# Local attention and a gated projection in one kernel: scores in four 64x64 products, transposes by 64 rows, three banks for dense work

## The chip, the cores and the metric

The kernel runs on one core of a Trainium2 chip. The metric is device time in microseconds (us) of one execution. Before the change it was 435.26 us, the median of 3 runs (435.07 to 436.68).

## The reference

Attention with batch 4, 8 heads, 768 positions and 64 features a head comes first. A query sees 31 neighbours (distance under 16) and 24 summaries, one for each 32 positions: the maximum of the keys and the mean of the values. A gated projection follows.

```python
k_sum = k.reshape(B, H, nb, block, D).max(axis=3)          # block 32
v_sum = v.reshape(B, H, nb, block, D).mean(axis=3)
scores_l = where(|i - j| < 16, q @ k.T / 8, -1e9)
scores_s = q @ k_sum.T / 8 + log(32)
a = softmax(concat([scores_l, scores_s])) ; attn = a @ concat([v, v_sum])
h = relu(x @ w_in)                                          # x: 4 x 768 x 512, w_in 512 x 1024
u, v = halves of h ; v_n = layer norm of v
v_s = w_spatial @ v_n + b_spatial[:, None]                  # w_spatial 768 x 768
out = (u * v_s) @ w_out                                     # w_out 512 x 512
```

The arithmetic is float32. Each dense product is made as three products of float32 values split into a high and a low part (hh, hl, lh), and w_in and w_out come in as 64-bit floats, which the kernel splits itself.

## The kernel before

**Attention.** The work is cut into 24 groups: 4 batches, 3 stretches of 256 queries (`c`), and 2 sets of four heads (`g`). A group has two head pairs (`pr`), and the two heads of a pair lie on partitions 0 to 63 and 64 to 127 (`a`). A stretch has four blocks of 64 queries (`BPU`), and a block is scored against 120 columns (`KW`): 64 keys, 24 summaries and 32 more keys. The steps of a group:

- `scores` (L410), once for each pair: for each block one product for each head, 64 features by 64 queries against 120 columns, so 8 products. TensorE runs each float32 product in two passes, and the profile shows 16 records for a pair and 32 for a group. The output of a pair is one PSUM bank (tile `s`; two such banks).
- softmax: per block VectorE (DVE) adds the mask and takes the extreme (L419), ScalarE (ACT) takes the exponent (L423), then come the sum's inverse (L428, L429) and the scaling (L431, on DVE or on GpSimd, called POOL).
- `trans` (L442), once for each pair: four transposes of 128 rows by 120 columns into one bank (tile `t`), copied to SBUF (tile `pt`) by ACT or DVE in one go (L229).
- `mix` (L458): 16 products with the values into tile `x`, one half of the output partitions for each head; 32 records.

**Dense work.** For each batch: `pv` (projection to v, 6 pieces), `pu` (to u, 8), `sp` (`w_spatial`, 8) and `po` (output, 6). All of their matmuls stand in one helper and have line L491. Each piece fills one bank of a pool of four (`m`), which ACT or DVE empties.

**What sets the order.** Nothing is left to a scheduler on the chip. The program lists operations with costs, and a planner (`Plan.order`) simulates the engines once, picks at each step the operation that can start first, and so writes the instruction order of every engine. The constants near the end steer it: `PACE` (time from group to group), `DENSE_0` and `STRETCH` (when dense pieces come due), `WIN_V` to `WO_AT` (weight loads), `FAVOUR` and `BUSY` (how far POOL is preferred over DVE for the operations that both can run), `RATE` and `WIRE` (speed and delay of loads). All loads go out on SyncE's queue. On the chip each engine runs its list strictly in order and waits where an input isn't there.

**The head of the program.** Keys, queries, values and the first half of w_in come in first; warming matmuls (`warm`) fill TensorE until there is work. `vsum` (L363) needs a 1.5 MB load of values (`vn`), and the first `mix` needs `vsum`.

**The end.** The last output piece is copied out of PSUM in two column halves of 256, first by DVE (L579) and then by ACT (L580), and goes out on two queues.

Of the kernel before, what the change touches and what calls it, by code (L numbers as in the profile page):

```python
# [63 lines left out]
class Plan:  # L64


    SLOTS = dict(s=2, t=1, x=1, m=4, k=4, vt=1, p=4, pt=3, x01h=2, x01l=2, x2h=2, x2l=2, g=NG, e=3, u=1, vnh=1, vnl=1,
                 gm=2, st=8, bs=4, mv=4)
# [6 lines left out]
    def add(self, engs, fn, pri, w=(), r=(), port=False, xfer=0):  # L75
# [103 lines left out]
def tile_local_summary_attention_gmlp(ctx: ExitStack, tc: tile.TileContext, qT, kext, vpad, vnat, vT, w_in, w_sp, b_rep, w_out, maskc, out):  # L179
# [220 lines left out]
    def scores(u, pri):  # L400
        b, c, pr = u
        ps = Buf(ps_s, [P, 512], F32, "s", f"s{b}_{c}_{pr}")
        kt, (qt, buf) = k_sb[b, pr], q_sb.pop(u)

        def mm(e):
            for i in range(BPU):
                g = c * BPU + i
                for a in range(2):
                    hs = slice(a * D, (a + 1) * D)
                    nc.tensor.matmul(  # L410
                        out=ps.t[hs, i * KW:(i + 1) * KW], lhsT=qt[hs, i], rhs=kt.t[hs, g * SEG:g * SEG + KW],
                        start=True, stop=True)
# [22 lines left out]
    def trans(u, pri):  # L435
        b, c, pr = u
        ps = Buf(ps_t, [P, 512], F32, "t", f"t{b}_{c}_{pr}")
        pt = p_sb.pop(u)

        def mm(e):  # L440
            for i in range(BPU):
                nc.tensor.transpose(out=ps.t[:KW, i * P:(i + 1) * P], in_=pt.t[:, i, :], identity=ident)  # L442
# [123 lines left out]
    def proj_out(b, t, pri):  # L566
# [8 lines left out]
        if (b, t) == (B - 1, NT - 1):  # L575
            hf = DM // 2

            def last(e):
                nc.vector.tensor_copy(out=ob.t[:, hf:], in_=ps.t[:, hf:])  # L579
                nc.scalar.copy(out=ob.t[:, :hf], in_=ps.t[:, :hf])  # L580
# [170 lines left out]
```

## Time and profile before

| | |
|---|---|
| median of 3 runs | 435.26 us |
| the profiled execution | 436.41 us, its span 434.6 us |
| mean granted TensorE clock | 0.995 |
| busy: TensorE matmul / weight load | 425.7 / 353.7 us |
| busy: DVE / ACT / POOL | 265.6 / 221.7 / 45.6 us |
| HBM read / written | 40.16 / 6.29 MB |

The span is the time from the first to the last instruction; 1.8 us of the profiled execution lie around it, and this execution took 1.15 us more than the median. In the profile PE is TensorE's matmul side and PEld its weight loads, which overlap it. A PE that is busy is not a PE at its peak: matmuls are pipelined, so what a block of work costs is read from the starts of the instructions around it.

### The profile page before, as it was taken

The page shows a single profiled execution, that of the slowest core. Times are in us where ns is not written, and L with a number is a line of the kernel's source. Part 1 is how long each engine was busy: PE and PEld are TensorE (multiplying, and loading weights), DVE is VectorE, ACT ScalarE, POOL GpSimd, SP SyncE. Part 2 cuts the span into 40 slices and gives each one's busy share as a digit, 9 for nine tenths or more (in the row PEclk, how much of TensorE's full clock was granted, in tenths as well). Part 3 has the DMA queues.
Part 4 walks back from the last instruction along what each step waited for, and adds up shares of the span by engine and source line. Part 5 has one row for each costly group of instructions (what it writes and reads, how often), then busy time and mean ns, then how long its engine had stood idle before and what let it go on. Part 6 is the DMA issues. An engine that isn't in the chain of part 4 may idle for free.

```text
span 434.6 us, 8979 instructions
## 1 busy us (share of the span) xinstructions
PE 425.7 (98%) x3374; PEld 353.7 (81%) x3374; DVE 265.6 (61%) x921; ACT 221.7 (51%) x668; POOL 45.6 (10%) x65
## 2 busy tenths in 40 slices
PE   8979999999999999999999999999999999999996
PEld 7637787788898888888888988789788988898885
DVE  4858999989993948455581657365482437143322
ACT  5658985874574546554273346375263254231121
POOL 1033611210001013010000002100000002010000
PEclk9989999999999999999999999999999999999999
DMA  8998967242155832320143251102103000000021
GB/s 288 362 271 289 296 205 247 76 133 60 26 165 161 250 118 60 106 67 26 38 144 118 87 186 27 38 24 62 38 26 109 26 36 15 0 2 0 2 97 48
DMA packets 25867, 47.03 MB, mean 108 GB/s; under 512 B 2528, under 2 KB 12896, under 8 KB 25696
## 3 DMA queue, kind: packets, MB, share of 16 engines
q1 hardware_dynamic: 25680, 46.33, 33.7%
q8 instruction: 26, 0.43, 0.4%
q14 instruction: 17, 0.14, 0.1%
q10 hardware_dynamic: 144, 0.13, 0.1%
HBM read 40.16 MB, written 6.29 MB: 107 GB/s over the span
## 4 chain that ended last, share of the span: by engine, by line
PE 82%; DMA 8%; DVE 8%; SPq 1%; issue 0%; ACT 0%; ACTq 0%
PE sp L491 24%; PE po L491 15%; PE pu L491 13%; PE pv L491 12%; PE s L410 8%; PE x L458 4%; PE t L442 4%; DMA vn<-in_vnat_dram 3%; DMA k<-in_kext_dram 2%; PE vsum L363 2%; DMA qd<-in_qT_dram 1%; DMA vt<-in_vT_dram 1%; DMA ws<-in_w_sp_dram 1%; DVE gm L342 1%; DVE p L419 1%; DVE p L431 1%
## 5 line engine op out<-in xcount | busy, mean ns | idle before, releaser
L423 ACT ACTIVATE p<-p,sums 128x120 f32<-128x120 f32 x192 | 73.6, 386 | 8.0 <-DVE sums L419 7.8
L491 PE MATMUL sp<-wsp_h,vnh 128*128 128x512 f32 (+1 forms) x192 | 66.7, 348 | 0.0
L491 PE MATMUL sp<-wsp_l,vnh 128*128 128x512 f32 (+1 forms) x192 | 64.7, 337 | 0.0
L491 PE MATMUL sp<-wsp_h,vnl 128*128 128x512 f32 (+1 forms) x192 | 64.6, 336 | 0.0
L419 DVE CUSTOM_DVE_ANT_0 p<-s,mask 128x120 f32<-128x120 f32 x192 | 42.8, 276 | 12.4 <-PE s L410 12.2
L491 PE MATMUL po<-wo_h,gt 128*128 128x512 f32 x128 | 47.7, 402 | 0.0
L410 PE MATMUL s<-k,qd 64*64 64x120 f32 x768 | 45.9, 267 | 0.5 <-DMA qd<-in_qT_dram 0.5
L410 PEld LDWEIGHTS s<-k,qd 64*64 64x64 f32 x768 | 39.1, 133 | 7.7 <-issue 4.4
L491 PE MATMUL pu<-xh,win_h 128*128 128x512 f32 (+1 forms) x128 | 44.7, 349 | 0.0
L491 PE MATMUL pu<-xh,win_l 128*128 128x512 f32 (+1 forms) x128 | 43.1, 337 | 0.0
L491 PE MATMUL pu<-xl,win_h 128*128 128x512 f32 (+1 forms) x128 | 43.1, 336 | 0.0
L562 ACT CAST gt<-g 128x512 fp32r<-128x512 f32 (+1 forms) x32 | 16.3, 513 | 50.2 <-DVE g L554 50.1
L491 PEld LDWEIGHTS sp<-wsp_h,vnh 128*128 128x128 f32 x192 | 36.4, 189 | 5.1 <-issue 1.3
L491 PE MATMUL pv<-win_h,xh 128*128 128x512 f32 x96 | 39.8, 414 | 0.0
L491 PEld LDWEIGHTS sp<-wsp_h,vnl 128*128 128x128 f32 x192 | 36.4, 189 | 3.9
L472 DVE TENSOR_TENSOR xl<-x,xh 128x512 fp32r<-128x512 f32 x24 | 16.4, 685 | 37.7 <-ACT xh L471 37.7
L491 PEld LDWEIGHTS sp<-wsp_l,vnh 128*128 128x128 f32 x192 | 36.4, 190 | 3.5
L491 PE MATMUL pv<-win_l,xh 128*128 128x512 f32 x96 | 37.6, 391 | 0.0
L491 PE MATMUL pv<-win_h,xl 128*128 128x512 f32 x96 | 37.5, 391 | 0.0
L491 PE MATMUL po<-wo_l,gt 128*128 128x512 f32 x96 | 37.5, 391 | 0.0
L553 DVE TENSOR_TENSOR g<-sp,brep 128x512 f32<-128x512 f32 (+1 forms) x32 | 17.7, 554 | 31.5 <-PE sp L491 22.1
L229 ACT COPY pt<-t 120x512 f32<-120x512 f32 x40 | 23.4, 584 | 26.1 <-PE t L442 25.9
(103 smaller groups left out, 784.7 us busy)
## 6 DMA issues: line engine op xcount, KB each, us to landing
k<-in_kext_dram SPq DMA_DIRECT2D x16, 544.0 KB, 5.8
qd<-in_qT_dram SPq DMA_DIRECT2D x24, 256.0 KB, 4.2
ve<-in_vpad_dram SPq DMA_DIRECT2D x24, 256.0 KB, 3.7
out_dram<-ob SPq DMA_DIRECT2D x23, 256.0 KB, 2.0
vt<-in_vT_dram SPq DMA_DIRECT2D x12, 384.0 KB, 4.0
wi<-in_w_in_dram SPq DMA_DIRECT2D x6, 512.0 KB, 5.1
ve<-in_vpad_dram SPq DMA_DIRECT2D x24, 128.0 KB, 3.4
wo<-in_w_out_dram SPq DMA_DIRECT2D x8, 256.0 KB, 5.4
```

What stands on the lines that cost most here:

```text
L229: (nc.scalar.copy if e == "ACT" else nc.vector.tensor_copy)(out=out_, in_=in_)
L342: nc.vector.tensor_reduce(out=g[:, :48].rearrange("p (s g) -> p s g", g=4), in_=kv[:, :, :QB].rearrange("p s (g e) -> p s g e", e=16), axi ...
L363: add(("PE", 860), lambda e, t=t, o=o: nc.tensor.matmul(out=ps.t[:SEG], lhsT=vs_in[:, o:o + SEG], rhs=vn.t[:, t, :], start=t == 0, stop=t ...
L410: nc.tensor.matmul(out=ps.t[hs, i * KW:(i + 1) * KW], lhsT=qt[hs, i], rhs=kt.t[hs, g * SEG:g * SEG + KW], start=True, stop=True)
L419: add(("DVE", 205), lambda e, i=i, mi=mi: nc.vector.tensor_tensor_reduce(out=pt.t[:, i, :], in0=ps.t[:, i * KW:(i + 1) * KW], in1=mask[:, ...
L423: add(("ACT", 380), lambda e, i=i: nc.scalar.activation(out=pt.t[:, i, :], in_=pt.t[:, i, :], func=AF.Exp, scale=-1.0, bias=st.t[:, 0, i:i ...
L442: nc.tensor.transpose(out=ps.t[:KW, i * P:(i + 1) * P], in_=pt.t[:, i, :], identity=ident)
L458: nc.tensor.matmul(out=ps.t[a * D:(a + 1) * D, r, n * QB:(n + 1) * QB], lhsT=ve[buf][:, n, o:o + D], rhs=tts[r].t[:, n * P + a * QB:n * P ...
L472: add(("DVE", 610), lambda e: nc.vector.tensor_sub(out=l.t[:, :, fs], in0=ps.t, in1=h.t[:, :, fs]), pri, w=[kl], r=[ps, kh, h, l])
L491: nc.tensor.matmul(out=ps.t[:, :n], lhsT=x, rhs=y, start=(j == i == 0), stop=(j == last and i == 2))
L553: add(("DVE", dve_ns(n)), lambda e: nc.vector.tensor_add(out=g.t[:, :n], in0=ps.t[:, :n], in1=brep[:, ts]), pri, w=[g], r=[ps, "brep"])
L562: add(("ACT", act_ns(n)), lambda e: nc.scalar.copy(out=gh[1](), in_=g.t[:, :n]), pri, w=[kh], r=[g, gt])
```

## The change

The four parts:

1. **Scores.** A group's two pairs are scored in one go. For each block there are four products in the order (head, pair) = (0,0), (1,1), (0,1), (1,0). The head sets the 64 rows of the array and the bank; the pair sets the 64 columns of the array and the 64 output partitions. Tile `s` is now two banks in a pool of one (it was one bank in a pool of two). The softmax takes one head of both pairs at a time.
2. **Transposes.** A softmax tile now holds pair 0 on rows 0 to 63 and pair 1 on rows 64 to 127. Each block is transposed as two products of 64 rows, which write 64 columns each to two banks, so there are 8 transposes where there were 4, per half group. The two copies to SBUF (120x512 as before) come after both halves.
3. **Banks.** Scores 2, transposes 2 (was 1), mix 1, dense pieces 3 (was 4).
4. **Plan.** New constants and costs (scores 1000 ns for a group, transposes 300 ns for a half group, mix 1050, loads at 330 GB/s), ten staging buffers for eight, some waits on staging buffers set earlier in `spatial`. The last output piece is cut by rows (64 and 64) and no longer by columns.

```diff
-    SLOTS = dict(s=2, t=1, x=1, m=4, ..., g=NG, ...)              # NG = 8
+    SLOTS = dict(s=1, t=1, x=1, m=3, ..., g=NG, ...)              # NG = 10
...
-    def scores(u, pri):
-        b, c, pr = u
-        ps = Buf(ps_s, [P, 512], F32, "s", f"s{b}_{c}_{pr}")
+    def scores(b, c, pg, buf, pri):
+        ps = Buf(ps_s, [P, 2, 512], F32, "s", f"s{b}_{c}_{pg}")
+        kts = [k_sb[b, 2 * pg + r] for r in range(2)]
+        qt = qd[buf]
...
-                for a in range(2):
+                for a, r in ((0, 0), (1, 1), (0, 1), (1, 0)):
                     hs = slice(a * D, (a + 1) * D)
                     nc.tensor.matmul(
-                        out=ps.t[hs, i * KW:(i + 1) * KW], lhsT=qt[hs, i], rhs=kt.t[hs, g * SEG:g * SEG + KW],
-                        start=True, stop=True)
-        add(("PE", 930), mm, pri, w=[ps], r=[kt, f"q{buf}"])
+                        out=ps.t[r * QB:(r + 1) * QB, a, i * KW:(i + 1) * KW], lhsT=qt[hs, r, i],
+                        rhs=kts[r].t[hs, g * SEG:g * SEG + KW], start=True, stop=True)
+        add(("PE", 1000), mm, pri, w=[ps], r=[*kts, f"q{buf}"])
+        for a in range(2):
+            softmax((b, c, pg, a), ps, pri)
...
-    def trans(u, pri):
-        ps = Buf(ps_t, [P, 512], F32, "t", f"t{b}_{c}_{pr}")
-                nc.tensor.transpose(out=ps.t[:KW, i * P:(i + 1) * P], in_=pt.t[:, i, :], identity=ident)
-        add(("PE", 450), mm, pri, w=[ps], r=[(pt, "n"), pt])
+    def trans(b, c, pg, pri):
+        ps = Buf(ps_t, [P, 2, 512], F32, "t", f"t{b}_{c}_{pg}")
+        for a in range(2):
+                    for r in range(2):
+                        hs = slice(r * QB, (r + 1) * QB)
+                        nc.tensor.transpose(out=ps.t[:KW, r, a * CH + i * QB:a * CH + (i + 1) * QB], in_=pt.t[hs, i, :], identity=ident[hs, hs])
+            add(("PE", 300), mm, pri, w=[(ps, a)], r=[(pt, "n"), pt, ps])
...
-                nc.vector.tensor_copy(out=ob.t[:, hf:], in_=ps.t[:, hf:])
-                nc.scalar.copy(out=ob.t[:, :hf], in_=ps.t[:, :hf])
+                nc.vector.tensor_copy(out=ob.t[D:], in_=ps.t[D:])
+                nc.scalar.copy(out=ob.t[:D], in_=ps.t[:D])
...
-PACE_0, PACE, DENSE_0, STRETCH = 12.13, 15.91, 66.3, 1.27
+PACE_0, PACE, DENSE_0, STRETCH = 12.13, 15.16, 59.674, 1.249
-FAVOUR, BUSY = 1380.0, 44480.0
-WIRE, RATE, RATE_64, RATE_32 = 1800, 375.0, 215.0, 195.0
+FAVOUR, BUSY = 1760.0, 55780.0
+WIRE, RATE, RATE_64, RATE_32 = 2200, 330.0, 210.0, 195.0
```

How the order moves, at three places. In the names, the batch is left out and the last number is the program's own: `s_0_0_2212` is the scores tile of stretch 0, set 0.

TensorE, the first scores of the third batch, before:

```order
L491 MATMUL pv_2_2076<-win_h,xl_01_1_1343 128x512
L410 MATMUL s_0_0_2098<-k_0_1633,qd_105 64x120 x8
L410 MATMUL s_0_1_2115<-k_1_1640,qd_105 64x120 x8
L380 MATMUL vmp_0_2125<-ident,vs_in 88x128
L380 MATMUL vmp_1_2127<-ident,vs_in 88x128
```

and after:

```order
L501 MATMUL pv_3_2189<-win_h,xl_01_1_1438 128x512
L411 MATMUL s_0_0_2212<-k_0_1866,qd_105 64x120
L411 MATMUL s_0_0_2212<-k_1_1877,qd_105 64x120 x2
L411 MATMUL s_0_0_2212<-k_0_1866,qd_105 64x120 x2
L411 MATMUL s_0_0_2212<-k_1_1877,qd_105 64x120 x2
L411 MATMUL s_0_0_2212<-k_0_1866,qd_105 64x120 x2
L411 MATMUL s_0_0_2212<-k_1_1877,qd_105 64x120 x2
L411 MATMUL s_0_0_2212<-k_0_1866,qd_105 64x120 x2
L411 MATMUL s_0_0_2212<-k_1_1877,qd_105 64x120 x2
L411 MATMUL s_0_0_2212<-k_0_1866,qd_105 64x120
L381 MATMUL vmp_0_2236<-ident,vs_in 88x128
```

Two blocks of 8 products became one of 16, in which the two pairs' keys take turns. No group's scores are parted any more, where five of the groups from the third on had other work between their two blocks.

TensorE, the transposes of the same group, before:

```order
L442 MATMUL t_0_0_2195<-ident,p_0_0_2136 120x128 x4
L491 MATMUL pu_0_1_2202<-xh_01_0_1193,win_h 128x512
L491 MATMUL pu_0_1_2202<-xl_01_0_1208,win_h 128x512
L491 MATMUL pu_0_1_2202<-xh_01_0_1193,win_l 128x512
L491 MATMUL pu_0_1_2202<-xh_01_0_1193,win_h 128x512
L491 MATMUL pu_0_1_2202<-xl_01_0_1208,win_h 128x512
L491 MATMUL pu_0_1_2202<-xh_01_0_1193,win_l 128x512
L442 MATMUL t_0_1_2213<-ident,p_0_1_2151 120x128 x4
```

and after:

```order
L450 MATMUL t_0_0_2309<-ident,p_0_0_0_2253 120x64 x8
L501 MATMUL pu_0_2_2303<-xh_01_0_1242,win_h 128x512
L501 MATMUL pu_0_2_2303<-xl_01_0_1252,win_h 128x512
L501 MATMUL pu_0_2_2303<-xh_01_0_1242,win_l 128x512
L501 MATMUL pu_0_2_2303<-xh_01_1_1422,win_h 128x512
L501 MATMUL pu_0_2_2303<-xl_01_1_1438,win_h 128x512
L501 MATMUL pu_0_2_2303<-xh_01_1_1422,win_l 128x512
L450 MATMUL t_0_0_2309<-ident,p_0_0_1_2268 120x64 x8
```

The halves of a group's transposes still stand apart with dense matmuls between them; each is 8 short ones in place of 4.

POOL, between the second group's softmax and the first layer norm, before (`wsp_l` is the low part of w_spatial, `mv` a layer norm's variance):

```order
L243 TENSOR_TENSOR wsp_l<-ws_0_311,wsp_h 128x512
L284 TENSOR_TENSOR win_l<-wf_2_0_347,wi_2_0_218 128x256
L431 TENSOR_TENSOR p_1_0_402<-p_1_0_402,sums 128x480
L431 TENSOR_TENSOR p_1_1_425<-p_1_1_425,sums 128x480
L431 TENSOR_TENSOR p_1_2_480<-p_1_2_480,sums 128x480
```

and after:

```order
L244 TENSOR_TENSOR wsp_l<-ws_512_347,wsp_h 128x256
L244 TENSOR_TENSOR wsp_l<-ws_0_362,wsp_h 128x512
L285 TENSOR_TENSOR win_l<-wi_0_429 128x512
L437 TENSOR_TENSOR p_2_0_0_648<-p_2_0_0_648,sums 128x480
L437 TENSOR_TENSOR p_2_0_1_671<-p_2_0_1_671,sums 128x480
L535 TENSOR_TENSOR mv_0_766<-mv_0_766,mhalf 128x1
L244 TENSOR_TENSOR wsp_l<-ws_512_370,wsp_h 128x256
L244 TENSOR_TENSOR wsp_l<-ws_0_379,wsp_h 128x512
```

POOL made one low part of w_spatial of the twelve before and makes eight now (five of 512 columns, three of 256); DVE makes the rest.

More of the change, by code (lines that the diff above doesn't have):

```diff
@@ L39 @@
 TH = 256
-NG = 8
+NG = 10
 EPS_LN = 1e-6
@@ L64 @@
 class Plan:
-    SLOTS = dict(s=2, t=1, x=1, m=4, k=4, vt=1, p=4, pt=3, x01h=2, x01l=2, x2h=2, x2l=2, g=NG, e=3, u=1, vnh=1, vnl=1,
+    SLOTS = dict(s=1, t=1, x=1, m=3, k=4, vt=1, p=4, pt=3, x01h=2, x01l=2, x2h=2, x2l=2, g=NG, e=3, u=1, vnh=1, vnl=1,
                  gm=2, st=8, bs=4, mv=4)
     TURNS = ("s", "t", "x", "k", "vt", "p", "pt", "gm", "e")
+    OUT_OF_TURN = ("wi", "wf", "wo", "ws", "ob")
     LAG = dict(PE=250, ACT=150, DVE=150, POOL=150, SP=0)
@@ L95, in add @@
         for x in (*w, *r):
-            if isinstance(x, Buf) and not x.ops and x.tag in self.TURNS and x.args[4][0] != "w" and x.args[4][:3] != "vmp":
+            if isinstance(x, Buf) and not x.ops and x.tag in self.TURNS and x.args[4][:2] not in self.OUT_OF_TURN :
                 self.turn.setdefault(x.tag, []).append(x)
@@ L104, in order @@
     def order(self):
-        free = {}
+        free = dict(SP=730)
         slots = {t: [(0, i) for i in range(n)] for t, n in self.SLOTS.items()}
@@ L387, in q_load @@
         dma(qd[buf], qT[b, c, g], 256, pri, w=[f"q{buf}"])
-        for r in range(2):
-            q_sb[b, c, 2 * g + r] = (qd[buf][:, r], buf)
     def v_load(b, c, g, buf, pri):
@@ L549, in spatial @@
         vh, vl, u = s["vh"], s["vl"], s["u"]
+        gt = Buf(moe, [P, 2 * TH], F32R, "g", f"gt{b}_{th}_{d}")
         mm3(ps, n, [((lambda k=k: vh.t[:, k, ds], lambda k=k: vl.t[:, k, ds], lambda k=k: wsp_h[:, k, ts], lambda k=k: wsp_l[:, k, ts]),
-                     [vh, vl, (vh, k), (vl, k), f"ws{k}_{ts.start}h", f"ws{k}_{ts.start}l"]) for k in range(NT)], pri)
+                     [vh, vl, (vh, k), (vl, k), f"ws{k}_{ts.start}h", f"ws{k}_{ts.start}l"]) for k in range(NT)], pri, *([gt] if th else []),
+            *([s["gl"][0, j][2] for j in range(NC)] if th and d >= NG - 8 else []))
         g = Buf(moe, [P, DF], F32, "e", f"g{b}_{th}_{d}")
@@ L617, in attention @@
                 key_prep(b, 2 * g + r, pri + KP_OFF + early(f"p{b}{g}{r}"))
-        for r in range(2):
-            scores((b, c, 2 * g + r), pri + early(f"s{i}{r}"))
+        scores(b, c, g, buf, pri)
         if b == c == g == 0:
@@ L624, in attention @@
                 vmean(b, 2 * g + r, pri, buf)
-        for r in range(2):
-            trans((b, c, 2 * g + r), pri + early(f"t{i}{r}"))
+        trans(b, c, g, pri)
         mix(b, c, g, buf, pri + early(f"x{i}"))
```

37 lines of the change are left out of this document (18 added, 19 removed).

## The prediction

> **What bounds the kernel now.** I read the page's busy shares and chain first, then a table of stretches, then the starts of TensorE's instructions around single blocks of attention work.
>
> ```profile
> span 434.6 us, 8979 instructions
> PE 425.7 (98%) x3374; PEld 353.7 (81%) x3374; DVE 265.6 (61%) x921; ACT 221.7 (51%) x668; POOL 45.6 (10%) x65
> PE 82%; DMA 8%; DVE 8%; SPq 1%; issue 0%; ACT 0%; ACTq 0%
> ```
>
> ```profile
> 0.00:33.60 33.60, 29.39 (x166) 19.82 (x167) 20.70 (x75) 19.34 (x56) 7.15 (x19) 0.95 0.94 309
> 33.60:45.00 11.40, 10.85 (x182) 9.37 (x181) 9.54 (x57) 11.03 (x40) 4.09 (x5) 1.00 0.91 279
> 45.00:100.00 55.00, 54.51 (x535) 44.49 (x534) 52.04 (x172) 43.18 (x130) 13.31 (x15) 1.00 0.60 187
> 100.00:130.00 30.00, 30.00 (x236) 25.62 (x236) 29.28 (x116) 17.35 (x64) 0.00 (x0) 1.00 0.26 81
> 130.00:358.00 228.00, 228.00 (x1876) 191.84 (x1878) 126.47 (x447) 111.87 (x347) 16.47 (x21) 1.00 0.27 83
> ```
>
> The columns of the table are length, then PE, PEld, DVE, ACT and POOL busy, the granted clock, DMA share and GB/s. Until 33.6 us the loads set the time (DMA 0.94). From there TensorE has next to no gap. From 45 to 130 us DVE is nearly full too (81.3 of 85 us); after 130 us it is at 55%, and only TensorE counts. So what a change saves on TensorE after 33.6 us shortens the run, if DVE keeps pace until 130.
>
> But busy time doesn't price a block, since matmuls overlap. Four blocks with the dense matmuls around them (start, length):
>
> ```profile
> 196.02 0.28 PE L491 MATMUL pu<-xl,win_h 128*128 128x256 f32 x1
> 196.14 0.28 PE L491 MATMUL pu<-xh,win_l 128*128 128x256 f32 x1
> 196.35 1.86 PE L410 MATMUL s<-k,qd 64*64 64x120 f32 x32
> 198.14 0.39 PE L491 MATMUL pu<-xh,win_h 128*128 128x256 f32 x1
> 198.36 0.28 PE L491 MATMUL pu<-xl,win_h 128*128 128x256 f32 x1
> ...
> 143.37 0.39 PE L491 MATMUL po<-wo_h,gu 128*128 128x512 f32 x1
> 143.69 1.04 PE L410 MATMUL s<-k,qd 64*64 64x120 f32 x16
> 144.66 0.39 PE L491 MATMUL sp<-wsp_h,vnh 128*128 128x256 f32 x1
> 144.88 0.28 PE L491 MATMUL sp<-wsp_l,vnh 128*128 128x256 f32 x1
> ...
> 185.16 0.39 PE L491 MATMUL pv<-win_l,xh 128*128 128x512 f32 x1
> 185.39 0.39 PE L491 MATMUL pv<-win_h,xl 128*128 128x512 f32 x1
> 185.62 0.60 PE L442 MATMUL t<-ident,p 128*120 128x128 f32 x4
> 185.97 0.48 PE L491 MATMUL pv<-win_h,xh 128*128 128x512 f32 x1
> 186.29 0.40 PE L491 MATMUL pv<-win_l,xh 128*128 128x512 f32 x1
> ...
> 189.74 0.40 PE L491 MATMUL pv<-win_h,xl 128*128 128x512 f32 x1
> 190.06 1.15 PE L458 MATMUL x<-pt,ve 120*64 120x64 f32 x32
> 191.15 0.50 PE L491 MATMUL pv<-win_h,xh 128*128 128x512 f32 x1
> 191.48 0.40 PE L491 MATMUL pv<-win_l,xh 128*128 128x512 f32 x1
> ```
>
> A block costs the time from the last dense start before it to the second one after it, less two dense steps (0.12 us at 256 columns, 0.23 at 512). That gives 198.36 - 196.14 - 0.24 = 1.98 us for a group's scores in one piece; 1.16 (144.88 - 143.37 - 0.23 - 0.12) for one pair's; 0.44 (186.29 - 185.39 - 0.46) for four transposes; 1.28 for a mix. The two scores blocks differ by 0.82 us for 16 records. Two heads run side by side, so that is 8 steps of 0.102 us, and a **fee** of 1.16 - 0.82 = 0.34 us is left for entering and leaving. The mix, a different cut of the array, has room for the same fee: (1.28 - 0.34) / 32 records = 0.029 us each. The transposes show none: 0.44 / 4 = 0.11 us, about the step of a full-array pass.
>
> **The change, part by part.** All sums are made against the profiled execution (436.41 us) for the 22 groups whose scores run after 33.6 us; the first two lie under the loads.
>
> Scores. Before: 17 groups in one piece at 1.98 and 5 parted at 2 x 1.16 = 2.32, together 45.3 us. After: 8 steps, each with four products side by side, and one fee. The lower bound of a step is today's 0.102 us. The nearest row for an upper bound, if TensorE has to feed records one by one, is the mix: 4 x 0.029 = 0.117. If only two products run at once, as now, a step is 0.205. I take 0.107, near the lower bound, since in the mix two column halves already run side by side and in the scores two row halves do: 8 x 0.107 + 0.34 = 1.20, times 22 is 26.4. **-18.9 us**; with 0.102, 0.117 and 0.205 it is -19.9, -17.2 and -1.7.
>
> Transposes. 46 half groups after 33.6 us cost 46 x 0.44 = 20.2 now. After, a half is 4 steps of two transposes with 64 columns each: half of 0.11 is 0.055 a step if both rows run at once and the weight loads keep up.
>
> ```profile
> L410 PEld LDWEIGHTS s<-k,qd 64*64 64x64 f32 x768 | 39.1, 133 | 7.7 <-issue 4.4 <-PE t L442 1.0 <-ACT k L352 0.8
> L442 PEld LDWEIGHTS t<-ident,p 128*120 128x120 f32 x192 | 22.6, 137 | 7.6 <-issue 2.5 <-POOL p L431 0.6 <-DVE p L431 0.4
> L491 PEld LDWEIGHTS sp<-wsp_h,vnl 128*128 128x128 f32 x192 | 36.4, 189 | 3.9
> ```
>
> A transpose's load of 120 columns lasts 137 ns, hardly more than 64 columns of scores (133) and far less than 128 dense ones (189), so I let it keep up. But 64-row transposes cut the array as scores and mix do, so I charge the fee: 43 visits in the new order (three pairs of halves stand together), 7 of them next to scores or mix at half a fee. That is 46 x 0.22 + 36 x 0.34 + 7 x 0.17 = 10.1 + 12.2 + 1.2 = 23.5: **+3.3 us**. Bounds: -10.1 with no fee; if a step stays at 0.11, +13.4.
>
> The Trainium skill's page "TensorEngine Tiling (Array Packing)", under Key Properties, says that a change of tiling mode drains TensorE. Scores and mix agree with it (0.34 us a visit); by it the transposes pay too, as in my sum, and without it the sum would be 13.4 us lower.
>
> Banks and staging buffers. Scores banks come free only when DVE has read both halves (8 operations, L419), but a group comes only every 15 us (`PACE`), so that wait is covered; three dense banks in place of four are covered as long as ACT and DVE empty a bank within two pieces. A wait of one 0.42 us DVE copy on each of the 32 shortest pieces (256 columns) would cost 13 us; I take 0, because after 130 us both engines are half idle. The mix is the same work: 0.
>
> The first stage, 33.6 to 130 us. TensorE would get about 4 us faster there (six groups of scores at 0.8, less 13 half groups at 0.07). DVE has 85 - 81.3 = 3.7 us free, and gives work to POOL:
>
> ```profile
> L243 DVE TENSOR_TENSOR wsp_l<-ws,wsp_h 128x512 fp32r<-128x512 f32 x5 | 3.4, 684 | 0.5 <-ACT wsp_h L242 0.5
> L243 DVE TENSOR_TENSOR wsp_l<-ws,wsp_h 128x256 fp32r<-128x256 f32 x6 | 2.5, 418 | 0.3 <-ACT wsp_h L242 0.3
> L243 POOL TENSOR_TENSOR wsp_l<-ws,wsp_h 128x512 fp32r<-128x512 f32 x1 | 1.4, 1445 | 0.0
> ```
>
> Four more of 512 and three of 256 columns make 4 x 0.68 + 3 x 0.42 = 4.0 us less on DVE; on POOL, idle for 70 of these 85 us, they take 8 or 9 us. Behind them on POOL wait the variances, and for those DVE. So DVE fits, with 3.7 us over. I take **+1 us** (bounds 0 and +4, all that this stage would win).
>
> The head. DVE's new list prepares all four keys before the first softmax. The last key's preparation ended at 21.7 us before, and the softmax of both groups must be through by the end of `vsum`:
>
> ```profile
> 20.57 0.95 DVE L342 TENSOR_REDUCE gm<-k 128x48 f32<-128x768 f32 x1 [1.22 <-DMA k<-in_kext_dram]
> 26.27 1.09 PE L363 MATMUL vsum<-vn,vs_in 128*88 128x512 f32 x2 [2.43 <-DMA vn<-in_vnat_dram]
> 27.89 5.89 PE L363 MATMUL vsum<-vn,vs_in 128*88 128x512 f32 x10
> L423 ACT ACTIVATE p<-p,sums 128x120 f32<-128x120 f32 x192 | 73.6, 386 | 8.0 <-DVE sums L419 7.8
> ```
>
> Sixteen exponents at 0.386 us from 22 us on end at 28.2; one scaling on POOL more is 29.2, and `vsum` ends at 33.6. I take 0; without that cover up to 2 us.
>
> The end. DVE's and then ACT's copy go from 256 columns to 512:
>
> ```profile
> 431.01 0.42 DVE L579 COPY ob<-po 128x256 f32<-128x256 f32 x1 [3.69 <-PE po L491]
> 431.51 0.37 ACT L580 COPY ob<-po 128x256 f32<-128x256 f32 x1 [2.59 <-DVE ob L579]
> ...
> L229 DVE COPY pt<-t 120x512 f32<-120x512 f32 x8 | 5.5, 681 | 2.3 <-PE t L442 2.3
> L229 ACT COPY pt<-t 120x512 f32<-120x512 f32 x40 | 23.4, 584 | 26.1 <-PE t L442 25.9
> ```
>
> ACT still waits for DVE in the new order: (0.68 - 0.42) + (0.58 - 0.37) = **+0.5 us**; if they ran at once, -0.2.
>
> Sum: 436.41 - 18.9 + 3.3 + 1 + 0.5 = 422.3. The profiled execution lies 1.15 us over the median, so against the runs shown it is **421.2 us**, 3.2% below 435.26.
>
> **The rivals.**
>
> *Transposes without a fee*, as the full-array ones show none today: -10.1 in place of +3.3, 407.8 us. Against it: scores and mix, both cuts of the array, pay the same 0.34.
>
> *Transposes held by their weight loads*: twice as many loads of 120 columns. If a step stays at today's 0.11, the term is +13.4: 431.3 us. For it: today's step may itself be the load's; against it: the short 137 ns. The Trainium skill's "TensorE: Matmul & The Clock Gate", under LDWEIGHTS, gives columns / 1.2 in ns, an estimate of 0.10 us for 120 columns, by which the sum would be some 2 us under this rival's. The rows differ from it: by that rule a load of 120 columns would last much longer than one of 64.
>
> *Slower: products that share columns of the array take turns.* Scores (0,0) and (0,1) use different columns, but (0,0) and (1,0), and the two transposes of a step, the same ones. Then a scores step is 0.205 (term -1.7), and a transposes step 2 x 0.055 (+13.4): 436.41 - 1.7 + 13.4 + 1.5 - 1.15 = 448.5 us. It decides once a scores step passes about 0.18: 22 x (8 x 0.18 + 0.34) = 39 us, some 6 under today's, which the other terms eat. For it: no row of this profile has two products on the same columns. Against it: they write different banks.
>
> *The scores don't go four wide, but the transposes do* (the change doesn't do what it says): -1.7 + 3.3 + 1.5, 438.4 us.
>
> **How the numbers follow.** Forecast 0.62 (its own range 417 to 427, from the bounds of the scores, first stage and head), no fee 0.12, loads 0.10, shared columns 0.08, not four wide 0.04; 0.04 for waits scattered by the new order that eat the gain and leave about 435. A measurement of this kernel can tell about 0.5% (2.2 us) from no change. Faster: 0.62 + 0.12 + 0.10 = 0.84; slower 0.12; same 0.04. The range 408 to 432 holds the forecast, the loads and half of the no-fee case.
>
> **What would show it.** Scores block after: 1.2 us by the same reading, four starts within some 0.02 us and steps of 0.10. A half group's transposes: 0.56 us, steps of 0.055. TensorE without gaps from 34 us on, DVE not fuller than 97% until 130. Wrong if scores steps are near 0.2, if transposes cost 0.22 or 0.78, or if PE shows waits of over 5 us in all after 34 us.

## The result, and the profile after

The changed kernel takes 428.39 us (median of 4 runs, 428.08 to 428.80), beside 435.16 (433.29 to 436.68) for the kernel before in the same series: ratio 0.985, 95% interval 0.981 to 0.989. It is 6.8 us faster; the forecast was 14.1 (435.26 to 421.2). The profiled execution took 428.28 us, 8.1 less than that of before, where the sum said 14.1 less. So some 6 us are missing, and the question is where.

The profile's first lines:

```profile
span 426.5 us, 9422 instructions
PE 413.7 (97%) x3604; PEld 333.0 (78%) x3604; DVE 269.2 (63%) x927; ACT 214.1 (50%) x655; POOL 52.8 (12%) x72
```

TensorE's blocks came out about as forecast. A group's scores and a half group's transposes with the dense matmuls around them, in the timeline of TensorE (start, length):

```profile
199.17 0.39 PE L501 MATMUL sp<-wsp_h,vnl 128*128 128x512 f32 x1
199.49 1.05 PE L411 MATMUL s<-k,qd 64*64 64x120 f32 x32
...
200.81 0.40 PE L501 MATMUL sp<-wsp_l,vnh 128*128 128x512 f32 x1
...
127.35 0.39 PE L501 MATMUL po<-wo_h,gu 128*128 128x512 f32 x1
127.67 0.45 PE L450 MATMUL t<-ident,p 64*120 64x64 f32 x8
...
128.39 0.40 PE L501 MATMUL po<-wo_l,gt 128*128 128x512 f32 x1
```

By the prediction's reading the scores cost 200.81 - 199.17 - 0.46 = 1.18 us a group (forecast 1.20), the transposes 128.39 - 127.35 - 0.46 = 0.58 us a half group (forecast 0.56).

What did not come out is the stretch up to 100 us. The table of stretches (length, then PE, PEld, DVE, ACT, POOL, the granted clock, DMA share, GB/s), first of before:

```profile
33.60:100.00 66.40, 65.36 (x716) 53.86 (x715) 61.59 (x228) 54.21 (x169) 17.40 (x20) 1.00 0.66 203
60.00:72.00 12.00, 12.00 (x87) 9.85 (x84) 11.10 (x30) 6.23 (x13) 0.55 (x1) 1.00 0.82 262
```

and of after:

```profile
33.60:100.00 66.40, 60.25 (x728) 47.39 (x725) 59.74 (x233) 52.41 (x176) 25.48 (x28) 0.95 0.75 197
60.00:72.00 12.00, 6.43 (x82) 4.84 (x82) 11.86 (x29) 6.95 (x14) 2.20 (x3) 0.74 1.01 278
```

TensorE, which had 1.0 us without work there, now has 6.2, nearly all of it between 60 and 72 us. How much work was done by 100 us is told by the same table for one line each, here before's dense matmuls (L491) and scores (L410),

```profile
33.60:100.00 66.40, 37.96 (x171) 28.11 (x172) 1.00 0.66 203
...
33.60:100.00 66.40, 13.44 (x224) 11.41 (x224) 1.00 0.66 203
```

and after's (L501, L411):

```profile
33.60:100.00 66.40, 39.34 (x168) 28.77 (x169) 0.95 0.75 197
...
33.60:100.00 66.40, 6.30 (x192) 4.93 (x192) 0.95 0.75 197
```

Before did 171 dense matmuls in this stretch, after 168, although its scores keep TensorE busy for 6.3 us in place of 13.4. (One scores group more lies ahead of 33.6 us now, hence 192 records; from 100 us on both have 480.) **At 100 us both kernels stand at the same point.** Scores, transposes, mixes and the projections done by then are the same; the fourth `sp` matmul (the 172nd dense one) starts at 100.20 us before and at 100.72 after:

```profile
100.20 0.40 PE L491 MATMUL sp<-wsp_h,vnh 128*128 128x512 f32 x1
...
100.72 0.40 PE L501 MATMUL sp<-wsp_h,vnh 128*128 128x512 f32 x1
```

This matmul is used below as the mark of the early part: from it to the end of the span it takes 334.4 us before and 325.7 after. What TensorE saved ahead of it turned into waiting:

```profile
60.51 1.05 PE L411 MATMUL s<-k,qd 64*64 64x120 f32 x32
64.71 0.31 PE L381 MATMUL vmp<-ident,vs_in 128*88 128x128 f32 x1 [3.15 <-ACT vf L528]
...
67.02 0.44 PE L381 MATMUL vmp<-ident,vs_in 128*88 128x128 f32 x1 [0.81 <-ACT ve L383]
69.07 0.79 PE L501 MATMUL pv<-win_h,xh 128*128 128x512 f32 x1 [1.60 <-ACT ve L383]
...
72.64 0.40 PE L501 MATMUL pv<-win_h,xl 128*128 128x512 f32 x1
72.89 0.40 PE L501 MATMUL pu<-xh,win_h 128*128 128x512 f32 x1
```

`vmp` waits for a bank that ACT empties into `vf`; ACT waits for a buffer that DVE's work on the second half of w_in holds (tile `win_l`); and the first `pu`, which needs that half, starts at 72.89 us. (The last `win_l` ends at 70.43 us. From there to `pu` TensorE is at work on the `pv` piece ahead of it, so what held TensorE were the buffer and the banks.) The rows of ACT and DVE:

```profile
64.06 0.60 ACT L528 ACTIVATE vf<-pv 128x512 f32<-128x512 f32 x1 [1.76 <-DVE win_l L285]
...
63.61 0.42 DVE L285 TENSOR_TENSOR win_l<-wf,wi 128x256 fp32r<-128x256 f32 x1
...
70.02 0.41 DVE L285 TENSOR_TENSOR win_l<-wf,wi 128x256 fp32r<-128x256 f32 x1
```

In the kernel before the same two stood here:

```profile
64.36 0.42 DVE L284 TENSOR_TENSOR win_l<-wf,wi 128x256 fp32r<-128x256 f32 x1
...
65.47 0.39 PE L491 MATMUL pu<-xh,win_h 128*128 128x512 f32 x1
```

DVE is 5.7 us later with that half, and `pu` 7.4 us.

### The profile page after: what moved, and what is told of

It is laid out like the page before. It is cut to its first block, busy times and chain, and to the rows that moved or that the text cites. A ratio compares the mean times of both kernels' runs of the same rounds, so it can differ in the third digit from the quotient of the medians.

```text
span 426.5 us, 9422 instructions
## 1 busy us (share of the span) xinstructions
PE 413.7 (97%) x3604; PEld 333.0 (78%) x3604; DVE 269.2 (63%) x927; ACT 214.1 (50%) x655; POOL 52.8 (12%) x72
## 4 chain that ended last, share of the span: by engine, by line
PE 90%; DMA 7%; ACT 1%; DVE 1%; POOL 0%; issue 0%; DVEq 0%; SPq 0%; POOLq 0%
PE sp L501 24%; PE pu L501 16%; PE po L501 16%; PE pv L501 14%; PE x L468 5%; PE s L411 5%; DMA ve<-in_vpad_dram 4%; PE t L450 3%; PE warm L670 3%; DMA ws<-in_w_sp_dram 2%; PE vsum L364 1%; PE wwi L280 1%; PE wwi L278 1%; PE vmp L381 0%; DVE p L425 0%; ACT ve L383 0%
## 5 line engine op out<-in xcount | busy, mean ns | idle before, releaser
L501 PE MATMUL sp<-wsp_h,vnh 128*128 128x512 f32 (+1 forms) x192 | 66.6, 347 | 0.0
L501 PE MATMUL sp<-wsp_l,vnh 128*128 128x512 f32 (+1 forms) x192 | 64.7, 337 | 0.0
L501 PE MATMUL sp<-wsp_h,vnl 128*128 128x512 f32 (+1 forms) x192 | 64.5, 336 | 0.0
L501 PE MATMUL po<-wo_h,gt 128*128 128x512 f32 x128 | 48.1, 404 | 0.0
L501 PE MATMUL pu<-xh,win_h 128*128 128x512 f32 (+1 forms) x128 | 44.7, 349 | 0.0
L501 PE MATMUL pu<-xl,win_h 128*128 128x512 f32 (+1 forms) x128 | 43.2, 337 | 0.0
L501 PE MATMUL pu<-xh,win_l 128*128 128x512 f32 (+1 forms) x128 | 43.0, 336 | 0.0
L501 PE MATMUL pv<-win_h,xh 128*128 128x512 f32 x96 | 41.0, 427 | 1.6 <-ACT ve L383 1.6
L501 PEld LDWEIGHTS sp<-wsp_h,vnh 128*128 128x128 f32 x192 | 36.3, 189 | 5.5 <-issue 1.1
L501 PEld LDWEIGHTS sp<-wsp_h,vnl 128*128 128x128 f32 x192 | 36.4, 190 | 4.0
L501 PEld LDWEIGHTS sp<-wsp_l,vnh 128*128 128x128 f32 x192 | 36.4, 190 | 3.5
L501 PE MATMUL pv<-win_l,xh 128*128 128x512 f32 x96 | 38.3, 399 | 0.0
L565 DVE TENSOR_TENSOR g<-sp,brep 128x512 f32<-128x512 f32 (+1 forms) x32 | 17.6, 552 | 32.7 <-PE sp L501 32.7
L501 PE MATMUL pv<-win_h,xl 128*128 128x512 f32 x96 | 38.0, 396 | 0.0
L501 PE MATMUL po<-wo_l,gt 128*128 128x512 f32 x96 | 37.6, 392 | 0.0
L429 ACT ACTIVATION_READ_ACCUMULATOR p<-p,sums 128x1 f32 x192 | 36.3, 189 | 0.0
L535 POOL TENSOR_TENSOR mv<-mv,mhalf 128x1 f32<-128x1 f32 x24 | 16.6, 694 | 135.4 <-DVE mv L533 127.8
L595 ACT COPY ob<-po 128x512 f32<-128x512 f32 x23 | 13.5, 587 | 33.8 <-PE po L501 28.2
```

Source lines behind the costliest of these rows:

```text
L429: add(("ACT", 380), lambda e, i=i: nc.scalar.activation(out=pt.t[:, i, :], in_=pt.t[:, i, :], func=AF.Exp, scale=-1.0, bias=st.t[:, 0, i:i ...
L501: nc.tensor.matmul(out=ps.t[:, :n], lhsT=x, rhs=y, start=(j == i == 0), stop=(j == last and i == 2))
L535: add(("POOL", 500), lambda e: nc.gpsimd.tensor_tensor(out=mv.t[:, 1:2], in0=mv.t[:, 1:2], in1=mhalf, op=ALU.pow), pri, w=[mv])
L565: add(("DVE", dve_ns(n)), lambda e: nc.vector.tensor_add(out=g.t[:, :n], in0=ps.t[:, :n], in1=brep[:, ts]), pri, w=[g], r=[ps, "brep"])
L595: add(("ACT", 520), lambda e: nc.scalar.copy(out=ob.t, in_=ps.t), pri, w=[ob], r=[ps])
```

## The experiments

Times are medians of 4 or 10 runs. The changed kernel (428.39) and the first runs with the kernel before stand in a series of their own; the kernel before had medians of 435.2 to 437.0 in the four series, so a difference between two series can be off by 1 or 2 us. Two runs that repeat the changed kernel's order up to 140 us (the one with thinned loads and the one with DVE's work added late) have their first `pu` at 72.2 and 71.9 us where the changed kernel has 72.9: a single execution's start can be off by 1 us. Short names: W, w_in's second half is late by its place in the plan; L, the loads are late; B, three dense banks are too few; D, up to 100 us DVE's work sets the pace.

### The loads, thinned

```diff
-        dma(lambda: st.t[:, :n], src, ...)
+        m = 32 if key in THIN else n             # THIN: the six later loads of w_spatial
+        dma(lambda: st.t[:, :m], src[:, :m], ...)
```

> The changed kernel with the same order on every engine, but the six loads of the spatial weights that are issued between 34 and 56 us carry 32 columns each, and their splits on ACT, DVE and POOL read the bias tile in their place (so the spatial weights of three of the six row blocks are left out, the work on them is not). Theory L (loads): TensorE's 8 us of loss between 60 and 70 us come from transfers that are late in a full queue and hold ACT's list; then the loss falls to some 2 us and the time to 422 to 423. Theory W (w_in's second half is late on DVE, because the plan keeps it behind POOL's work, and holds buffers, banks and the first pu piece): only ACT's own wait of 1.3 us for such a load can go; TensorE still loses 6 to 8 us between 60 and 70, and the time is 427 to 428.5.

Measured: 428.01 us (427.22 to 428.30). The stretch of the wait, and what TensorE waits for:

```profile
60.00:72.00 12.00, 7.10 (x67) 5.46 (x59) 11.79 (x29) 6.37 (x13) 2.73 (x4) 0.65 0.66 216
...
PE vmp L383 <- ACT vf L530: 3.2, 1, 3.2
```

The DMA share falls from 1.01 to 0.66, and the waits stay. L falls: full queues were there, but nothing waited for them that something else didn't hold as well.

### w_in's second half, earlier in DVE's list

```diff
-        add(("DVE", n * 0.72 + 60), ..., port=True)
+        add(("DVE", n * 0.72 + 60), ..., port=key[:3] != "wi0")   # and the other three kinds
```

> The changed kernel, but in the plan DVE's operations on w_in's second half (four kinds, the rest of the rules as they are) no longer wait until POOL is free, so that they stand some 5 us earlier in DVE's list. Theory W: the first pu piece starts near 66 us (72.9 in the changed kernel, 65.5 in the one before), TensorE's loss between 60 and 70 us falls to 3 us or less, and the time to 422 to 424. Theory L: the loads are as late as before, so the time stays at 427 or more, and the loss stays within 1.5 us of 8.

Measured: 429.43 us (428.61 to 429.82). The first `pu` starts at 69.4 us instead of 72.9, but TensorE now waits elsewhere, between 36 and 56 us:

```profile
PE x L468 <- DVE xl L482: 2.8, 1, 2.8
PE x L468 <- ACT pt L230: 2.5, 1, 2.5
```

So putting this work first in DVE's list is no remedy: something else is late then, and by 100 us the same 168 dense matmuls are done. It doesn't show that DVE's order is without effect (the run with the scores alone, below, has the old order). This led to theory D.

### Transposes of 128 rows again

```diff
-                    for r in range(2):
-                        nc.tensor.transpose(out=ps.t[:KW, r, a * CH + i * QB:...], in_=pt.t[hs, i, :], identity=ident[hs, hs])
+                    nc.tensor.transpose(out=ps.t[:KW, a, i * P:(i + 1) * P], in_=pt.t[:, i, :], identity=ident)
```

> The changed kernel with the same order, but a half group's transposes are four of 128 rows in one bank in place of eight of 64 rows in two; scores stay four wide. If the price of 0.586 us a half group is that of the cut (0.446 without it) and only what comes after the loss at 60 to 70 us counts, 36 halves times 0.14 give 5.0 us less, 423.4; if all 46 count, 422.0. If the price is not that of the cut, 428.4 as now.

Measured: 424.10 us (423.69 to 424.26), 4.3 less than the changed kernel: the cut of the array has its price, as forecast, and it counts mostly after the loss: of 4.1 us in the span 3.2 lie behind the fourth `sp` matmul. It is 0.7 us less than 36 x 0.14, because the halves that stand beside scores or in pairs share a visit: in the changed kernel a half beside scores adds 0.38 us to the block, and two halves together cost 0.82.

### Scores two at a time

```diff
-                for a, r in ((0, 0), (1, 1), (0, 1), (1, 0)):
+        for i, pair in [(i, pair) for pair in (((0, 0), (1, 1)), ((0, 1), (1, 0))) for i in range(BPU)]:
+                for a, r in pair:
```

> The changed kernel with the same order of pieces, but a group's scores go through one diagonal pair of quarters first and the other after it, two at a time in 16 steps instead of four at a time in 8. A group then costs 1.98 us again in place of 1.18. If what TensorE saved before the loss at 60 to 70 us was lost there anyway, only the 17 groups after it count: 428.4 + 17 x 0.80 = 442.0. If every group since 33 us counts, 446. If the steps do not depend on how many quarters are busy, 428.4.

Measured: 437.24 us (436.12 to 437.99): 8.9 more, where 13.6 or 17.6 were expected. The price of a block was wrong:

```profile
203.67 0.39 PE L501 MATMUL sp<-wsp_h,vnl 128*128 128x512 f32 x1
...
203.99 1.51 PE L411 MATMUL s<-k,qd 64*64 64x120 f32 x32
...
205.77 0.40 PE L501 MATMUL sp<-wsp_l,vnh 128*128 128x512 f32 x1
```

The scores last 1.51 us, not the 1.86 of before (quoted in the prediction) and not the 1.05 of four at a time, and the block costs 1.64. The single records show why: the second diagonal's first product starts 0.47 us after the first one's, before the first diagonal's last three steps. Products of different quarters pass each other here. With 0.46 us a group, 17 groups make 7.8 and 22 make 10.1. The 15 groups behind the fourth `sp` matmul cost 6.8 us in the profiled execution, as they should (15 x 0.46 = 6.9), and the early ones 2.3 of 3.2, so part of the early groups counts when TensorE gets slower.

### DVE's work on w_in's second half, thinned

```diff
+        k = 32 if key[:3] == "wi0" else n
-            out=fi(), in0=words(1), ...
+            out=fi()[:, :k], in0=words(1)[:, :k], ...                  # and the other four kinds
```

> The changed kernel with the same order, but DVE's operations on w_in's second half (the shift, the sign, the mask, the low words, the subtraction) work on 32 columns in place of 256 or 512; the first half of the projected features is left wrong by it, no other work is. From the durations in the trace this takes 5 to 6 us off DVE between 33 and 70 us, some 2.5 of them before 60. Theory D (the stage up to 72 us ends when DVE has got through the work that is due by then, so what TensorE saves there is waited away): the first pu piece starts 4 to 5.5 us earlier than 72.9, TensorE's loss between 60 and 70 us falls by as much, and the time is 423 to 424.5. Theory B (three dense banks and three buffers for the normalised rows stop TensorE, whatever DVE's load): the same pieces wait for the same buffers, the loss falls by 1.5 us at most, 427 or more.

Measured: 426.37 us (424.14 to 426.69); the profiled execution is the one of 424.14. There the first `pu` starts 5.1 us earlier, and by 100 us 186 dense matmuls are done in place of 168, 4.1 us of work at 0.227. The fourth `sp` matmul starts 4.1 us earlier (96.61), and from it to the end it takes 325.7 us, as in the changed kernel:

```profile
67.83 0.63 PE L502 MATMUL pu<-xh,win_h 128*128 128x512 f32 x1
...
33.60:100.00 66.40, 43.39 (x186) 31.90 (x186) 0.97 0.65 199
```

In place and size that is theory D; the median, 2.0 us less, lies between the two. The other three executions took 2.0 to 2.6 us more than the profiled one, at a granted clock of 0.990 to 0.991 over the span where it had 0.995. An estimate from these figures: 0.0045 of 422 us are 1.9 us, so the clock can account for most of this; where it fell in them no trace shows.

### Four banks for dense pieces

```diff
-    SLOTS = dict(s=1, t=1, x=1, m=3, ...)        # t: two banks
+    SLOTS = dict(s=1, t=1, x=1, m=4, ...)        # t: one bank for each half group, 128-row transposes
```

> The run with the 128-row transposes in this order (424.1 us), but with one bank for the transposes in place of two and so four banks for dense pieces, and the plan worked out anew with that. Theory B: the wait of 3 us at vmp for a bank goes, and with it most of the 7.3 us that TensorE loses between 60 and 70 us: 419 to 421. Theory D: what is late is DVE's work, so TensorE waits somewhere else between 35 and 75 us: 423 to 426.

Measured: 423.87 us (422.37 to 424.62), as with three banks (424.10). The wait at `vmp` is gone, and others stand in its place, for the same engines' work:

```profile
PE x L466 <- DVE xl L480: 2.2, 1, 2.2
PE t L450 <- DVE pt L230: 1.6, 1, 1.6
```

B falls, at least with this order: four banks remove the wait for a bank and gain 0.2 us.

### The scores alone, on the kernel before

```diff
-    def scores(u, pri):                                           # one pair
+    def scores(b, c, pg, pri):                                    # both pairs
...
+                for a, r in ((0, 0), (1, 0), (0, 1), (1, 1)):
+                    hs, os = slice(a * D, (a + 1) * D), slice((a ^ r) * D, ((a ^ r) + 1) * D)
+                        out=ps.t[os, r, i * KW:(i + 1) * KW], lhsT=qts[r][hs, i], rhs=kts[r].t[hs, ...]
```

> The kernel before, its plan's numbers, its four dense banks, its transposes of 128 rows and its last piece as they were; only a group's four sets of scores go through the four quarters together (the second pair's heads swap their halves of the rows so that all four quarters are used). By TensorE's blocks alone 22 x 1.18 = 25.9 in place of 45.3 us: 435.2 - 19.4 = 415.8, if the first stage takes its part. Theory D: the five groups before 72 us gain nothing there, so 435.2 - 15.4 = 420. If the changed kernel's loss came from its new plan alone, no wait of TensorE over 1 us is left between 33 and 72 us here.

Measured: 423.05 us (422.69 to 424.77), in its series 0.969 of the kernel before (0.964 to 0.975). It beats the changed kernel by 5.3 us with one of its four parts. Its stretch from 33.6 to 100 us, its longest wait there, its first `pu` and its fourth `sp` matmul:

```profile
33.60:100.00 66.40, 62.01 (x725) 50.41 (x724) 64.43 (x241) 55.75 (x175) 15.82 (x19) 1.00 0.68 201
...
61.95 0.39 PE L496 MATMUL pu<-xh,win_h 128*128 128x512 f32 x1
...
95.91 0.28 PE L380 MATMUL vmp<-ident,vs_in 128*88 128x128 f32 x1 [1.47 <-DVE vs_in L376]
...
98.95 0.39 PE L496 MATMUL sp<-wsp_h,vnh 128*128 128x512 f32 x1
```

Between 33 and 72 us no wait is over 0.9 us, the granted clock stays at 1.00, and the first `pu` starts 3.5 us before that of the kernel before. By the condition set beforehand the loss between 60 and 72 us thus goes with the new plan, which sets the order of DVE and of the other engines: under that plan neither the old transposes nor the old transposes and banks together removed it (first `pu` at 72.2 and 70.5). But the saving isn't kept. The 145th dense matmul is 4.0 us earlier than in the kernel before (88.97 against 93.02), the fourth `sp` only 1.25: between them TensorE waits 2.2 us, first for DVE's `vs_in` at 95.9 us. DVE is now busy for 64.4 of 66.4 us (97%). So with the old plan too, DVE sets the time near 100 us, at another place and with less loss. Behind the fourth `sp` matmul the run is 12.3 us faster than the kernel before, about 15 x 0.80. Against the 435.2 us of the first series the gain is 12.1, against 437.0 of its own 13.9; theory D's 15.4 is nearer to it than 19.4, and still too much.

### The same with six numbers of the plan moved

```diff
-WIN_V, WIN_U, WSP_AT, WO_AT = -7.07, 47.63, 54.52, 99.2
-VT_OFF, VM_OFF, KP_OFF = 7.67, 6.61, -9.44
+WIN_V, WIN_U, WSP_AT, WO_AT = -7.332, 47.63, 67.849, 105.415
+VT_OFF, VM_OFF, KP_OFF = 6.355, 7.218, -6.466
```

> The same as the one before in this list, with six of the plan's numbers moved (loads of the spatial weights 13 us later in rank, those of the output weights 6, the keys' preparation 3 us later, two of the values' 1 us, and 1090 ns for a group's scores). Theory D leaves room for a better order of DVE's early work: 1 to 4 us below the run with the old numbers, 414 to 418. If the first stage is at its floor whatever the order, the same time within 1 us.

Measured: 423.11 us (418.61 to 423.89). The median is the same, so the 1 to 4 us that theory D left room for were not found with these numbers. One execution was 4.2 us faster, at a granted clock of 1.000 where the others had 0.992 to 0.996; what it did otherwise no trace shows.

### DVE's work added: early, late, and in the kernel before

```diff
-            nc.vector.tensor_reduce(out=g[:, :48]..., in_=kv[:, :, :QB]..., axis=AX.X, op=ALU.max)
+            for _ in range(3 if b == 1 and pr < 2 else 1):        # the late run: b == 2
+                nc.vector.tensor_reduce(out=g[:, :48]..., in_=kv[:, :, :QB]..., axis=AX.X, op=ALU.max)
```

> The changed kernel with the same order, but on DVE the large maximum over a key tile (0.87 us from start to start) is worked three times in place of once for the second batch's first two keys, near 53 to 58 us: 3.5 us more work for DVE there, and nothing else. Theory D (up to 100 us the run goes at DVE's pace): the first pu piece starts 3 to 3.5 us later than 72.9, and the time rises by 2.5 to 3.5, to 431 to 432. If DVE had room there, as the prediction took it (3.7 us free up to 130 us), it rises by 1 us at most.

Measured: 431.40 us (429.44 to 433.61), 3.0 more. In the profiled execution (432.16) the first `pu` is 3.05 us later and the fourth `sp` 3.9 (104.63); from there on it takes 325.7 us, as in the changed kernel:

```profile
75.94 0.63 PE L502 MATMUL pu<-xh,win_h 128*128 128x512 f32 x1
```

> The same 3.5 us more on DVE, but for the third batch's first two keys, near 150 us, where DVE is busy for 60% of the time. Theory D: no change, 428.4 within 1 us. If any work of DVE counts, wherever it stands, 431 to 432 as in the run before.

Measured: 429.48 us (429.30 to 429.66), 1.1 more: a third of what the same work costs early, and just over what theory D allowed. Beside the run before, in the same series, it is 1.9 us less. It isn't free, though: from the fourth `sp` matmul on the profiled execution takes 327.2 us, 1.5 more than the changed kernel. Two waits stand where the work stands, and the changed kernel has none there:

```profile
152.31 0.45 PE L451 MATMUL t<-ident,p 64*120 64x64 f32 x8 [0.45 <-DVE p L438]
156.90 1.50 PE L469 MATMUL x<-pt,ve 120*64 120x64 f32 x32 [0.56 <-ACT pt L230]
```

> The kernel before the change with the same 3.5 us more for DVE at the same keys, near 56 to 58 us. Its TensorE had no gap there. Theory D in its full form (DVE set the pace up to 100 us in the kernel before too, TensorE only just kept up with it): 2 to 3.5 us more than the kernel before in the same series. If TensorE alone set the pace there, 1 us more at most.

Measured: 439.96 us (437.27 to 440.88 in nine of ten executions, 444.50 in one), 4.7 more than the kernel before in its series (435.22); ratio 1.010 (1.006 to 1.014). The profiled execution's span is 3.4 us longer, and all of it lies ahead of the fourth `sp` matmul (103.61). TensorE, which had no gap there, now waits for DVE, and 1.7 us at 60.6 us for the keys, whose preparation the added work lengthens:

```profile
PE t L443 <- DVE p L432: 3.4, 2, 3.2
```

Together: 3.5 us of DVE's work cost 3.0 us in the changed kernel and 4.7 in the kernel before if they stand near 55 us (3.9 and 3.4 in the profiled executions), and 1.1 if they stand near 150; 5 to 6 us less of it there bring 2 to 4. That DVE's early work sets the time is shown, and for the kernel before too: its full TensorE only just kept up with DVE. The other half of theory D, that later work of DVE costs nothing, is not borne out. The added work stands in the keys' preparation, so a part of its price may be the keys' delay and not DVE's load; the thinned work doesn't touch the keys. ACT, 95% busy from 33.6 to 60 us in the changed kernel (96% before), may have a part in it; no run tested that by itself.

### Fillers for TensorE's waits

```diff
+    def fill(n):
+        for _ in range(n):
+            nc.tensor.matmul(out=s_ps[1, 0, 0].t[:, 0, BPU * KW:], lhsT=ident, rhs=ident[:, :512 - BPU * KW], start=True, stop=True)
```

> The changed kernel with 23 small matmuls of 32 columns put into TensorE's list in the three waits between 61.5 and 69 us (14, 3 and 6), into columns of a scores bank that nothing reads. They take no wait away; they only keep TensorE at work. In the changed kernel the granted clock falls to 0.50 from 66 to 72.7 us and eight dense matmuls take 0.43 us from start to start in place of 0.23. If the clock falls because TensorE stood idle, it stays near 1.0 here and the time falls by 1.5 to 2 us, to 426.5; if it falls for another reason, or the fillers are in the way, 428.4 or up to 1 us more.

Measured: 428.02 us, but from 425.43 to 431.03. The clock (the column before the DMA share) in one microsecond, in the changed kernel, then in the run with DVE's work added late, then with the fillers in the profiled execution (425.43):

```profile
66.00:67.00 1.00, 0.21 (x4) 0.02 (x2) 1.00 (x4) 0.95 (x3) 1.00 (x2) 0.50 1.00 253
...
66.00:67.00 1.00, 0.12 (x1) 0.00 (x0) 1.00 (x2) 1.00 (x3) 0.77 (x1) 0.50 0.84 301
...
66.00:67.00 1.00, 0.99 (x10) 0.88 (x9) 1.00 (x2) 0.88 (x2) 0.77 (x1) 1.00 0.70 241
```

With the fillers the clock stays at 1.00 from 60 to 73 us and the dense matmuls keep their 0.23 us from start to start. The run with the late work is the fair comparison: up to there it has the changed kernel's order, and `vmp` and the last `win_l` start within 0.01 us of the times with the fillers (63.40 and 63.39, both 68.71). In it the clock stands at 0.50 from 63.0 to 73.3 us, and the first `pu` starts at 71.87 us; with the fillers it starts at 69.47. So in these two traces TensorE's idleness is what lowered the clock, and it cost 2.4 us. The Trainium skill's "TensorE: Matmul & The Clock Gate" (Part 1) says that the clock halves after at least one idle window of about 3.4 us. The two traces agree only roughly: both waits lasted 3.15 us, and the clock fell 4.3 us (changed kernel) and 2.8 us (late work) after they had begun. Whether the fillers help on the whole stays open: two of the four executions took over 428.8 us, at a granted clock of 0.985, and no trace shows where theirs fell.

## Why the prediction was wrong

The direction was right, and so was the mechanism on TensorE. The steps, all against the profiled executions:

| step | forecast | shown |
|---|---|---|
| scores, 22 groups | -18.9 | 22 x 1.18 - 45.3 = -19.3 in TensorE's blocks |
| transposes, 46 half groups | +3.3 | about +4.5 (with the 128-row form the 32 half groups behind the fourth `sp` matmul took 3.2 less; 46 in proportion 4.6) |
| banks, staging, mix | 0 | 0 (four banks in place of three: -0.2) |
| first stage | +1 | about +5.6, what is left of the sum |
| end | +0.5 | +1.1 |
| sum | -14.1 | -8.1 |

**Scores.** Right: a step is 0.102 us, four products start within 0.02 us, and the block costs 1.18. The two rivals on this (columns that take turns, not four wide) fall with it.

**Transposes.** Right in kind, and about 1 us too low: the cut pays a fee at each visit. (0.58 - 0.34) / 4 is 0.06 us a step, near the 0.055 taken; the rivals with no fee and with loads that hold the step fall.

**The first stage: the step that failed.** The prediction let the saving ahead of 100 us count in full and took back 1 us, on the ground that "DVE fits, with 3.7 us over". By its own terms that saving is 7 / 22 of 18.9 less 14 / 46 of 3.3, 5.0 us. What came of it is nothing: at the fourth `sp` matmul the changed kernel is 0.5 us behind. Four things were wrong with the step. The room was summed over 85 us, while TensorE needs w_in's second half and the first batch's softmax by 65 us; in the changed kernel DVE has 0.14 us free from 60 to 72 us. That TensorE was at 98% was read as "TensorE sets the time", where the runs with added work show that DVE set it as well, in the kernel before too. The saving itself was miscounted: "six groups" and "13 half groups" up to 130 us are 9 (288 records) and 18 (72 records) in the trace of before. And nothing was said of DVE's order. From 33.6 us until it is through with `win_l`, DVE is busy (third column) for 28.7 us before and 33.7 after:

```profile
33.60:64.78 31.18, 30.50 (x403) 25.25 (x402) 28.74 (x120) 28.57 (x97) 12.08 (x13) 1.00 0.84 259
...
33.60:70.43 36.83, 30.68 (x449) 23.02 (x446) 33.71 (x130) 30.69 (x104) 20.22 (x21) 0.94 1.04 270
```

In its new list two rows of statistics, a normalisation and its low part, a copy of transposes, a split of the mix, a sum of values and two subtractions of w_in more stand ahead of `win_l`, and only 2 us of `wsp_l` less. These 5.0 us and 0.7 us more of idling are the 5.7 us by which `win_l` is late. That the wait between 60 and 72 us comes of this list is borne out by three profiled executions: less DVE work in it gave back 4.1 us of span, more took 3.9, and with the old plan's list the wait is not there. How much of the loss is the list's and how much DVE's total load no run separates.

The early loss adds up. The saving in blocks ahead of the mark is 4.7 us by the table's right column (7 / 22 of 19.3 less 14 / 46 of 4.5), the head gave 2.0 (below), and the mark comes 0.5 us late: 7.2 us lost. Against it stand 5.2 us more of waiting (6.2, before 1.0) and 1.75 us for eight matmuls at half clock, 6.9. Under "waits scattered by the new order" the prediction had such a case with a chance of 0.04, and as a loss of the whole gain; here about 6 of 14 us are missing. The range 408 to 432 nevertheless holds the time; that is luck and no sign for the path, since the forecast's own range was 417 to 427, and the wider one takes in a rival that fell (transposes held by their loads, 431.3).

The work on POOL did not come free either: while POOL works on `wsp_l`, a DVE operation that takes 0.29 us at 60.6 us took 1.36.

```profile
66.55 1.53 POOL L244 TENSOR_TENSOR wsp_l<-ws,wsp_h 128x512 fp32r<-128x512 f32 x1
...
66.87 1.36 DVE L268 TENSOR_SCALAR wi<-wf 128x256 int32<-128x256 int32 x1
```

**From 100 us on** the sum holds roughly. Priced one by one in the way of the prediction, the blocks there cost 65.9 us before and about 56.0 after, -9.9, and from the fourth `sp` to the last matmul it takes 9.7 us less (430.59 - 100.20 against 421.41 - 100.72). By the prediction's terms it would have been -10.6; the transposes are most of the difference.

**The end** was mis-sized. From the last matmul's start to the end of the span it takes 5.1 us, before 4.0:

```profile
421.41 0.39 PE L501 MATMUL po<-wo_h,gt 128*128 128x512 f32 x1
...
423.18 0.55 ACTq L592 DMA_DIRECT2D out_dram<-ob  x1
```

In the kernel before:

```profile
430.59 0.39 PE L491 MATMUL po<-wo_h,gt 128*128 128x512 f32 x1
...
431.91 0.38 ACTq L582 DMA_DIRECT2D out_dram<-ob  x1
```

The engines' part is 0.45 us (1.77 against 1.32 to the last issue), as forecast; the other 0.6 us lie in the issue and the transfer of 64 rows, which the prediction left out. The run with the scores alone keeps the old end and needs 4.0 us.

**The head** did no harm: `vsum` ended at 31.8 us, 2.0 earlier than before (27.89 + 5.89 = 33.78, where the prediction read 33.6). What this gave was lost before 100 us with the rest.

## What to carry to other kernels

An engine at 98% is not proof that it alone sets the pace: where a second engine is nearly full in the same stretch (DVE had 93% from 33.6 to 100 us), ask what of its work is due when, and add or take a few us of it in one run before pricing a saving there. Price a saving stage by stage, and count it only where the other engines have room at that moment, not on average. And of a change in four parts, try the strongest alone: here the scores by themselves, with the old transposes, banks and plan, were 5 us better than the whole.

## What the hardware showed that was not expected

Products of different quarters of the array passed each other: with the diagonals one after the other, the second began three steps before the first was through, and a group took 1.51 us in place of 1.86. And TensorE paid twice for a wait of about 3 us: the clock stood at 0.50 for 6.8 us in one execution and 10.2 in another, and in the first eight dense matmuls took 3.57 us (69.07 to 72.64) in place of 1.82.
